# Talking-heads attention and a squared-ReLU FFN on one core: a new static schedule, 16-bit scaling of q, in-place ReLU, joined copies

## The chip, the core and the metric

The kernel runs on one core of one Trainium2 chip. Its engines each work off a queue of their own in program order: TensorE (PE: matmuls; its weight loads appear as PEld), VectorE (DVE), ScalarE (ACT), GpSimd (POOL) and SyncE (SP, which here only issues DMAs). They meet through semaphores. TensorE writes PSUM, which the kernel uses as eight banks of 128 x 512 fp32; DVE and ACT empty it into SBUF. The metric is the device time of one execution in microseconds.

## What is computed

```python
def _attn_ref(q, k, v, w_pre, w_post):              # q, k, v: (8, 12, 448, 64); w: (12, 12)
    scale = 1.0 / np.sqrt(q.shape[-1])
    scores = scale * np.matmul(q, k.transpose(0, 1, 3, 2))
    scores = np.einsum('bhij,hg->bgij', scores, w_pre)
    scores = scores - np.max(scores, axis=-1, keepdims=True)
    attn = np.exp(scores)
    attn = attn / (np.sum(attn, axis=-1, keepdims=True) + 1e-09)
    attn = np.einsum('bhij,hg->bgij', attn, w_post)
    return np.matmul(attn, v)

def reference(...):
    x = attn_out.transpose(0, 2, 1, 3).reshape(3584, 768)
    h = np.maximum(x @ w_in, 0.0)                   # w_in: (768, 2048), w_out: (2048, 768)
    return h * h @ w_out
```

Heads are mixed twice, once ahead of the softmax (`w_pre`) and once behind it (`w_post`).

## The kernel before

The eight batch entries are worked off one behind the other, each in these steps, which overlap with those of its neighbours:

- **T**: q and k come by DMA (issued by POOL, `load_qk`) and are transposed on TensorE (`emit_T`, L726) into `qkt`.
- **Scores**: for each pair of heads and 128 rows of q a score tile of 448 columns (`emit_QK`, L879) is copied from PSUM to `stage` (L486 on ACT, L487 on DVE: the helper `copy` does all plain copies), and a DMA (`emit_rel`, SP, L925) puts it in another order, with 5 rows x 12 heads on 60 partitions, into `dring`.
- **pre**: one small matrix on TensorE mixes the heads (`emit_pre`, L948). For the first 22 groups of ten rows of batch 0 the mix is made otherwise, without the DMA: DVE multiplies q by the 12 factors of `w_pre` (`emit_scale`, L802, "scaling"), and TensorE adds up the heads (`emit_direct`, L824).
- **Softmax**: ACT takes the exponential into `pring` and the row sums (`after_pre`, L965). DVE takes the reciprocal (`rinv`, L979). A **fold** multiplies the second mix's matrix `wk2b` by it into `wk2s` (L986), and a **tail** multiplies 64 columns of a pair's exponentials by it into `ptail` (L1001). `pring`, `wk2s` and `rinv` are rings of `NPS = 10`.
- **post**: the second mix, transposed at the same time (`emit_post`, L1036, L1050); its results leave PSUM as `a2t`.
- **AV** (L1120) gives `xt`. **F1** (L1176 in full rows, L1184 in half rows) gives the hidden layer: a ReLU from PSUM into one of three buffers `h1t` (L1213 on ACT, L1214 on DVE), then DVE squares it into `h2t` (L1223). **F2** (L1251 for the last tiles, L1303 full, L1311 half rows) gives the output through `osb` and a DMA that POOL issues (L1348).

TensorE uses its array in four forms: full (128 x 128), half rows, half columns, and quarters of 64 x 64, of which two or four run at once. Where TensorE would idle early on, the plan adds matmuls that compute nothing (L599).

The order on every engine is made ahead of time, while the program is built, by a planner (`_Plan.run`). It holds a list of tasks with their inputs, a cost for each engine that may do a task, and a priority. TensorE's tasks stand in ten streams (T, QK, pre, post, AV, direct, F1 twice, F2 twice), and the string `ORDER` says digit by digit which stream comes next. Tasks of engine `FLEX` go to ACT or DVE, wherever they would end first by the plan. A task of TensorE takes the PSUM banks that come free first. What stands in the order by the plan stays in that order on the chip; an engine waits at a task whose inputs are late, and all behind it with it. The plan's times come from constants:

```python
SEM_LAT = 60.0
MODE_SWITCH = 106.0                     # TensorE changes its array form
t_fold = add(..., DVE if g < 10 else POOL, fn_fold, ..., {POOL: (330.0, 370.0), DVE: (200.0, 280.0)}, ...)
```

`F1_FULL`, `F2_FULL`, `QK_QUAD` and `POST_QUAD` say, unit by unit, which array form is used.

Of the kernel before, what the change touches and what calls it, by code (L numbers as in the profile page):

```python
# [17 lines left out]
SEM_LAT = 60.0  # L18
MODE_SWITCH = 106.0
ACT_BIAS = 14.5  # L20
BLOCK = 256
# [11 lines left out]
    "0010155055051505511551555115555113553155550033555555550105555555311553332550220555315551"  # L33
    "2313332431244123622317667223677313361372267113667313242244137611376713127721266676623336"
    "7277128310028323839139229839200223444132622008111811181338317222167663123776313673132621"
    "4431411367217127766327621002677622383383338162267720028332677102208311813181338314212442"
    "2229391139313933922291444229119116316337221763363372217620016733722631620027137383200281"
    "1181118222939133911393124222441183138311831382224442216363372217633637212763362002277200"
    "2611637337339200292219119118131813183318222444223931193139331922244422881383138336221672"
    "1276200167337136336222772002736316720209119313922193831183138113822244422381381338224442"  # L40
    "2816336117117336221673373621167200226731362002713783382228382002911392219139393319222931"
    "9318338111811382224444442236171163377331722166662227637336372127922198338392298333832244"
    "42228876323267886673363363676787774448687787766676697767689989889999"
)
F1_FULL = "1111111111111111111111111111111100000000000001000000010000000110001010001111011111111111"
F2_FULL = "00000000000000000000000000101100"
QK_QUAD = "001000000001000000000000000000000000000000001001000000010000001000000000000000000000000000000000000000000000000000000000000000000000000000000000000000000000000"
POST_QUAD = "0000000000000000000000000000000000000000000000000000000000000000000000000000000000000000000000000000000000000000000000000000000000000000000000000000000000000000000000000000000001100000"
# [48 lines left out]
class _Group:  # L97


    __slots__ = ("n", "banks", "readers")  # L100

    def __init__(self, n):
        self.n = n
        self.banks = None
        self.readers = [[] for _ in range(n)]


class _Plan:
# [28 lines left out]
    def start(self):  # L137
        for t in self.tasks:
# [3 lines left out]
            for d in t.deps:  # L142
                if d.done:
                    t.avail = max(t.avail, d.end + SEM_LAT)
                else:
                    t.nwait += 1
                    d.succs.append(t)
# [50 lines left out]
    def _finish(self, t):  # L198
        t.done = True
        for s in t.succs:  # L200
            s.nwait -= 1
            spare = MARGIN.get((t.dma[0], s.engine), (0.0, 0.0)) if t.dma else (0.0, 0.0)
            s.avail = max(s.avail, t.end + SEM_LAT + spare[0 if t.end < 110e3 else 1])
# [53 lines left out]
    def bank_time(self, i):  # L257
        return max([t.end + SEM_LAT if t.done else INF for t in self.bank_users[i]] + [0.0])

    def find(self, n, now):  # L260
        best = sorted((max(self.bank_time(i), now), self.bank_age[i], i)
                      for i in range(len(self.bank_users)))
        return best[n - 1][0], [x[2] for x in best[:n]]
# [12 lines left out]
    def _commit_pe(self, t, start):  # L276
# [3 lines left out]
        if g is not None and g.banks is None:  # L280
            _, got = self.find(g.n, self.free[PE])
# [18 lines left out]
    def next_unit(self, order, at):  # L300
# [6 lines left out]
        if t.group is not None and t.group.banks is None:  # L307
            est = max(est, self.find(t.group.n, self.free[PE])[0])
# [43 lines left out]
def bass_talking_heads_attention__then__ffn_squared_relu_kernel(  # L352
# [45 lines left out]
    with ExitStack() as es:  # L398
# [7 lines left out]
        NPS = 10  # L406
        NOS = 2
        OP = F // 4
        NH1 = 3
# [10 lines left out]
        wq = sb("wq", [128, NP, H], DT.float32)  # L420
        wall = sb("wall", [128, NP, 2, H], DT.float32)
        mask2 = sb("mask2", [128, 2, H5], DT.float32)
# [6 lines left out]
        sb("align", [128, 224], DT.uint8)  # L429
# [13 lines left out]
        h1t = sb("h1t", [128, NH1, S], DT.bfloat16)  # L443
# [24 lines left out]
        def c_pe(t):  # L468
            return {PE: (t, t + 190.0)}
# [4 lines left out]

        def add(name, engine, fn, deps, cost, prio, mode=None, group=None, instrs=0):
            return plan.add(name, engine, fn, deps, cost, prio, "ctr", 1, mode, group=group,
# [11 lines left out]

        streams = [[] for _ in range(10)]
# [6 lines left out]
        def fn_init(eng, en):  # L496
# [4 lines left out]
            eng.memset(mask2[:, :, :], 1.0)  # L501
# [28 lines left out]
        t_m = select("init6", mask2, [[-64, 2], [-H, H5]], 0, 1, [t_init], -1e7 + 22)  # L530
        t_m = select("init7", mask2, [[64, 2], [H, H5]], H - 1, -1, [t_m], -1e7 + 23)
        t_mask2 = halves("init8", mask2, [t_m], -460.0)
# [13 lines left out]
        def fn_wsmall(eng, en):  # L546
            src = bass.AP(w_pre.tensor, 0, [[0, CH], [H, H], [1, H]])
            eng.dma_start(wrep[R0:R0 + NR, :], src).then_inc(sem_w0.handle, 16)
            for x in range(2):
                src = bass.AP(w_post.tensor, 0, [[0, H5], [H, H], [1, H]])  # L550
# [11 lines left out]
        for kk in range(2):  # L562
            def fn_wq(eng, en, r0=kk * 64, kk=kk):
                return eng.tensor_scalar(wq[r0:r0 + 64, :, :], wall[r0:r0 + 64, :, kk, :],
                                         scale, None, op0=ALU.mult)

            wq_of.append(add("wq%d" % kk, DVE, fn_wq, [t_wall], {DVE: (150.0, 220.0)}, -2e6))

        def fn_wk1(eng, en):
            o = wk1[:, 0:PR].rearrange("p (a b) -> p a b", b=H)  # L570
            i0 = wrep[:, :].unsqueeze(1).to_broadcast([128, H5, H])
            i1 = mask[:, 0, :].unsqueeze(2).to_broadcast([128, H5, H])
            return eng.scalar_tensor_tensor(o, i0, scale, i1, op0=ALU.mult, op1=ALU.mult)

        def fn_wk2(eng, en):
            r_ = None
            for x in range(2):
                r0, r1 = 64 * x, 64 * x + PR
                i0 = wrep2[r0:r1, :].unsqueeze(2).to_broadcast([PR, H, H5])
                i1 = mask2[r0:r1, 0, :].unsqueeze(1).to_broadcast([PR, H, H5])  # L580
# [6 lines left out]
        def warm_up(gap):  # L587
# [19 lines left out]
            start = max(now, t_warm.end + SEM_LAT, plan.find(1, now)[0])  # L607
# [102 lines left out]
        def emit_T(b):  # L710
            pb = b % 2
            for a in range(3):
                g = _Group(2)
# [767 lines left out]
```

## Time and profile before

| | us |
|---|---|
| three runs | 518.17, 518.59, 519.81 |
| their median | 518.59 |
| the profiled execution: from its first to its last instruction | 519.3 |
| TensorE busy in it | 506.3 |
| ACT, DVE, POOL busy | 434.1, 401.9, 268.4 |

The list of runs doesn't say which of them was profiled; its span lies 0.7 us above the median and 0.5 below the slowest. TensorE's granted clock was 1.00 throughout. In rows of the timeline a start and a duration in us stand first, then engine, line, operation and tiles; a bracket tells how long the engine had been idle and whom it waited for. In grouped rows (`x80 | 30.0, 405 | 1.9`) stand the count, busy us, mean ns of one, and idle us ahead. In rows of stages, `20.00:40.00`, the busy us of PE, PEld, DVE, ACT and POOL stand behind the length, with counts in brackets. In rows of waits stand the sum in us, the times and the longest. Rows of one operation that follow each other are merged: the duration of a merged row is that of all, and operations on one engine overlap a little, so the time from start to start is less than the mean of one.

### The profile page before, as it was taken

How to read it: one execution, taken by the hardware profiler on the slowest of the kernel's cores; microseconds unless marked ns; L12 is line 12 of the kernel's file. 1: busy time of each engine (PE TensorE's matmuls, PEld its weight loads, DVE VectorE, ACT ScalarE, POOL GpSimd, SP SyncE). 2: the span in 40 equal slices, each digit the busy share in tenths (PEclk: the TensorE clock that was granted, in tenths of full speed). 3: DMA queues.
4: the chain of work that ended last, by engine and by line, in shares of the span. 5: the costliest groups of instructions: out<-in, count | busy, mean ns of one | idle time of the engine just before them, and what ended most of it. 6: DMA issues, size and time to landing. Idle time of an engine off the chain costs nothing.

```text
span 519.3 us, 22377 instructions
## 1 busy us (share of the span) xinstructions
PE 506.3 (98%) x9169; PEld 319.7 (62%) x9169; DVE 401.9 (77%) x1025; ACT 434.1 (84%) x1256; POOL 268.4 (52%) x571
## 2 busy tenths in 40 slices
PE   7999899999999999999999999999999999999997
PEld 3455677567776664567455664566545665568884
DVE  8998999689979769888988869886896668755220
ACT  4989999799999898988888889888998888987531
POOL 9956556443673576244864459235664344443000
PEclk9999999999999999999999999999999999999999
DMA  8999999846895689646993679626995466551013
GB/s 112 196 227 193 199 180 189 168 115 136 157 190 135 142 174 187 124 97 141 173 186 76 142 156 197 148 66 152 174 166 119 102 154 120 103 118 32 1 32 93
DMA packets 83022, 72.33 MB, mean 139 GB/s; under 512 B 7160, under 2 KB 80424, under 8 KB 82920
## 3 DMA queue, kind: packets, MB, share of 16 engines
q0 software_dynamic: 37632, 33.83, 40.4%
q1 hardware_dynamic: 45000, 36.86, 29.0%
q8 instruction: 74, 1.21, 0.9%
q14 instruction: 28, 0.23, 0.1%
q10 hardware_dynamic: 288, 0.20, 0.1%
HBM read 47.27 MB, written 11.01 MB: 112 GB/s over the span
## 4 chain that ended last, share of the span: by engine, by line
PE 73%; DVE 12%; ACT 8%; DMA 3%; issue 2%; POOL 2%; POOLq 0%; ACTq 0%; DVEq 0%
PE ps L1311 23%; PE ps L1184 10%; PE ps L1176 10%; PE ps L1120 6%; PE ps L948 6%; PE ps L879 5%; PE ps L1036 5%; ACT pring L965 4%; PE ps L1303 3%; DVE stage L487 3%; DVE a2t L487 2%; PE ps L1251 2%; DMA kraw<-in_k_dram 2%; DVE w_out_sb L802 2%; PE ps L726 2%; ACT stage L486 2%
## 5 line engine op out<-in xcount | busy, mean ns | idle before, releaser
L965 ACT ACTIVATE pring<-ps 128x448 bf16<-128x448 f32 x360 | 191.7, 557 | 11.7 <-PE ps L948 9.4
L986 POOL TENSOR_TENSOR wk2s<-wk2b,rinv 128x120 bf16<-128x120 bf16 (+1 forms) x179 | 73.2, 409 | 145.7 <-DVE rinv L979 144.3
L487 DVE CAST a2t<-ps 128x420 bf16<-128x420 f32 (+1 forms) x208 | 124.8, 643 | 16.5 <-PE ps L1050 15.9
L1311 PE MATMUL ps<-w_out_sb,h2t 64*128 64x384 bf16 x1472 | 134.3, 323 | 0.3 <-ACT pring L965 0.2
L487 DVE CAST stage<-ps 128x448 bf16<-128x448 f32 (+1 forms) x179 | 107.3, 615 | 14.1 <-PE ps L879 12.8
L486 ACT ACTIVATE a2t<-ps 128x420 bf16<-128x420 f32 (+1 forms) x160 | 94.9, 645 | 13.1 <-PE ps L1050 12.8
L486 ACT ACTIVATE stage<-ps 128x448 bf16<-128x448 f32 (+1 forms) x181 | 94.8, 557 | 12.9 <-PE ps L879 12.2
L1311 PEld LDWEIGHTS ps<-w_out_sb,h2t 64*128 64x128 bf16 x1472 | 67.6, 94 | 45.3 <-issue 2.4
L1184 PE MATMUL ps<-xt,w_in_sb 64*128 64x448 bf16 (+1 forms) x840 | 88.4, 347 | 1.3 <-issue 1.1
L1348 POOL DMA_DIRECT2D out_dram<-osb x52 | 33.4, 648 | 93.3 <-ACT osb L486 30.7
L965 ACT ACTIVATION_READ_ACCUMULATOR pring<-ps 128x1 f32 x360 | 80.0, 222 | 0.0
L1176 PE MATMUL ps<-xt,w_in_sb 128*128 128x228 bf16 (+2 forms) x636 | 75.0, 270 | 1.0 <-ACT a2t L486 0.8
L1223 DVE TENSOR_TENSOR h2t<-h1t 128x448 bf16<-128x448 bf16 (+2 forms) x176 | 56.0, 341 | 20.2 <-ACT h1t L1213 17.1
L1001 POOL TENSOR_TENSOR ptail<-pring,rinv 128x128 bf16<-128x128 bf16 x171 | 70.2, 410 | 0.0
L1176 PEld LDWEIGHTS ps<-xt,w_in_sb 128*128 128x128 bf16 x636 | 58.2, 98 | 13.9 <-ACT a2t L486 1.7
L1036 PEld LDWEIGHTS ps<-wk2s,pring 60*128 60x128 bf16 (+1 forms) x2184 | 48.9, 94 | 24.7 <-issue 2.6
L1184 PEld LDWEIGHTS ps<-xt,w_in_sb 64*128 64x128 bf16 x840 | 37.5, 94 | 34.8 <-issue 2.2
L1213 ACT ACTIVATE h1t<-ps 128x448 bf16<-128x448 f32 (+2 forms) x100 | 43.5, 445 | 16.6 <-PE ps L1176 7.6
L1036 PE MATMUL ps<-wk2s,pring 60*128 60x60 bf16 (+1 forms) x2184 | 55.3, 187 | 1.3 <-ACT h1t L1213 0.6
L948 PE MATMUL ps<-dring,wk 64*64 64x448 bf16 (+1 forms) x676 | 54.0, 362 | 0.9 <-DVE a2t L487 0.3
L979 DVE RECIPROCAL rinv<-rowsum 128x2 f32<-128x2 f32 (+1 forms) x184 | 29.0, 157 | 32.9 <-ACT pring L965 31.5
L879 PE MATMUL ps<-qkt 64*128 64x448 bf16 (+1 forms) x372 | 51.1, 353 | 0.4 <-DVE qkt L487 0.3
(62 smaller groups left out, 564.1 us busy)
## 6 DMA issues: line engine op xcount, KB each, us to landing
dring<-stage SPq DMA_DIRECT2D x309, 105.0 KB
out_dram<-osb POOLq DMA_DIRECT2D x52, 192.0 KB, 4.0
vraw<-in_v_dram POOLq DMA_DIRECT2D x48, 128.0 KB
qraw<-in_q_dram POOLq DMA_DIRECT2D x48, 112.0 KB, 5.4
kraw<-in_k_dram POOLq DMA_DIRECT2D x48, 112.0 KB, 5.3
w_in_sb<-in_moe_w_in_dram POOLq DMA_DIRECT2D x8, 384.0 KB, 18.0
w_out_sb<-in_moe_w_out_dram POOLq DMA_DIRECT2D x8, 384.0 KB, 17.3
dring<-stage SPq DMA_DIRECT2D x30, 42.0 KB
```

Of the source, the lines that this page charges most:

```text
L486: return eng.activation(o, i_, AF.Copy)
L487: return eng.tensor_copy(o, i_)
L879: r_ = eng.matmul(ps[y * v:(y + 1) * v, g.banks[x], 0:S], qkt[r0:r0 + 64, pp, 0, j0:j0 + v], qkt[r0:r0 + 64, pp, 1 + pb, :], start=True, s ...
L948: r_ = eng.matmul(ps[64 * y:64 * y + 64, gr.banks[x], 0:S], wk1[64 * x:64 * x + 64 - R0 * x, :], dring[64 * x:64 * x + 64 - R0 * x, (g0 + ...
L965: return eng.activation(pring[:, pr, 0:S], ps[:, gr.banks[x], 0:S], AF.Exp, accum_out=rowsum[:, pr, :])
L986: return eng.tensor_tensor(wk2s[:, p0:p0 + n, :], i0.to_broadcast([128, n, PR]), rinv[:, p0:p0 + n, :].to_broadcast([128, n, PR]), ALU.mult)
L1001: return eng.tensor_tensor(ptail[:, p0 // 2, :, :], pring[:, p0:p0 + 2, 0:PJ], rinv[:, p0:p0 + 2, :].to_broadcast([128, 2, PJ]), ALU.mult)
L1036: r_ = eng.matmul(ps[z * v:(z + 1) * v, gr.banks[x], o0:o0 + PR], pring[64 * x:64 * x + PR, pr + y, c:c + v], wk2s[64 * x:64 * x + PR, pr ...
L1176: r_ = eng.matmul(ps[:, gs[ph].banks[0], 0:n], w_in_sb[:, ft, t * 128:(t + 1) * 128], xt[:, ft, c0:c1], start=(ft == 0), stop=(ft == NFT - 1))
L1184: r_ = eng.matmul(ps[:, gs[0].banks[x], 0:n], w_in_sb[64 * y:64 * y + 64, ft, t * 128:(t + 1) * 128], xt[64 * y:64 * y + 64, ft, c0:c1], s ...
L1223: return eng.tensor_tensor(h2t[:, t16, o0:o0 + n], h1t[:, s, 0:n], h1t[:, s, 0:n], ALU.mult)
L1311: r_ = eng.matmul(ps[:, gs[0].banks[hh], 0:FH], h2t[64 * y:64 * y + 64, t16, col:col + 128], w_out_sb[64 * y:64 * y + 64, t16, hh * FH:(hh ...
```

## The change

1. **Scaling of q in 16 bits.** The factors `wq` were fp32, one for each head, read with a step of 0; they are now bf16 and written out five times, and the product's columns stand in the order head, row instead of row, head. `wk1`, `mask2` and the loads of the weights follow that order; two of POOL's selections for `mask2` become two sums on DVE.
2. **In-place ReLU.** `h1t` goes; the ReLU writes `h2t`, and the square is taken there. The wait for the F2 of the batch before, which had stood at the square, stands at the ReLU.
3. **Joined copies.** A unit of TensorE may take two neighbouring banks (`_Group(2, True)`), and one instruction then empties both. The squares of a pair may be one instruction too.
4. **Folds and tails** may be on POOL or DVE, as the plan finds better, with 120 ns to DVE's disadvantage; before, those of the first ten groups were on DVE and all others on POOL.
5. **The planner's constants** are other ones, and `ORDER` and the strings of forms are new (`ENG_V` is all zeros and changes nothing). `NPS` goes from 10 to 12.

```diff
-SEM_LAT = 60.0
-MODE_SWITCH = 106.0
+LAT = {PE: 85.0, ACT: 32.0, DVE: 32.0, FLEX: 32.0, POOL: 78.0, SP: 60.0}
+DMA_LAT = 60.0
+MODE_SWITCH = 97.0
+FOLD_BIAS = 120.0
...
-    "0010155055051505511551555115555113553155550033555555550105555555311553332550220555315551"
+    "0010155505115500551155555555331555511355001155400155555315553315552355555550203552135551"
...
-        NPS = 10
+        NPS = 12
...
-        wq = sb("wq", [128, NP, H], DT.float32)
+        wq = sb("wq", [128, NP, H, H5], DT.bfloat16)
...
-                            "p (c a) -> p c a", a=H5).unsqueeze(3).to_broadcast(
-                            [128, 2 * n, H5, H])
-                        i1 = wq[:, p, :].unsqueeze(1).unsqueeze(1).to_broadcast(
-                            [128, 2 * n, H5, H])
+                            "p (c a) -> p c a", a=H5).unsqueeze(2).to_broadcast(
+                            [128, 2 * n, H, H5])
+                        i1 = wq[:, p, :, :].unsqueeze(1).to_broadcast(
+                            [128, 2 * n, H, H5])
...
+    def find(self, n, now, side=False):
+        if side:
+            t = [max(self.bank_time(i), now) for i in range(len(self.bank_users))]
+            e = min((max(t[i], t[i + 1]), max(self.bank_age[i], self.bank_age[i + 1]), i)
+                    for i in range(len(t) - 1))
+            return e[0], [e[2], e[2] + 1]
...
+        def two(g, c, dt=None):
+            a = g.banks[0]
+            return (ps if dt is None else dt)[:, a:a + 2, 0:c]
...
-            t_fold = add("fold%d_%d" % (b, c), DVE if g < 10 else POOL, fn_fold,
+            t_fold = add("fold%d_%d" % (b, c), FLEX, fn_fold,
                          [t_rec, t_wk2] + old_users(g),
-                         {POOL: (330.0, 370.0), DVE: (200.0, 280.0)},
+                         {POOL: (345.0, 391.0), DVE: (200.0, 283.0)},
...
+            t_fold.bias = FOLD_BIAS
...
+            def emit_relu(x, k, g, z):
+                h = h2t[:, t16 + x:t16 + x + k, o0:o0 + n]
+
+                def fn_relu(eng, en):
+                    i_ = two(g, n) if k == 2 else ps[:, g.banks[z]:g.banks[z] + 1, 0:n]
+                    if en == ACT:
+                        return eng.activation(h, i_, AF.Relu)
+                    return eng.tensor_scalar(h, i_, 0.0, None, op0=ALU.max)
+
+                t = add("relu%d_%d_%d" % (b, c0, t16 + x), FLEX, fn_relu,
+                        [ths[x if full else 1]] + free, c_ev(k * n), b * 1000.0 + 600)
```

Three places of the new order, by engine. In them `qkt` is the transposed q or k, `stage` the scores, `pring` the exponentials, `wk2s` a fold and `ptail` a tail; `w_out_sb` lends its space to the scaled q until its own weights are loaded.

DVE at the start of the program, from the factors of q to the sixth scaling, before:

```order
L564 TENSOR_SCALAR wq<-wall 64x72 x2
L487 COPY qkt<-ps 128x448
L802 TENSOR_TENSOR w_out_sb<-qkt,wq 128x8x60 x2
L487 COPY qkt<-ps 128x448
L802 TENSOR_TENSOR w_out_sb<-qkt,wq 128x8x60 x2
L487 COPY qkt<-ps 128x448 x2
L802 TENSOR_TENSOR w_out_sb<-qkt,wq 128x8x60 x2
```

and after:

```order
L617 TENSOR_SCALAR wq<-wall 64x360 x2
L579 TENSOR_REDUCE mask<-ident 60x5 x2
L528 COPY qkt<-ps 128x448
L864 TENSOR_TENSOR w_out_sb<-qkt,wq 128x8x60 x4
L528 COPY qkt<-ps 128x448
L864 TENSOR_TENSOR w_out_sb<-qkt,wq 128x8x60 x2
L528 CAST stage<-ps 128x448
```

The factors are wider, two sums stand ahead of the first copy of q, and four scalings instead of two ahead of the second copy.

ACT in the middle of batch 0's direct scores, behind its last plain copy of `qkt`, before:

```order
L486 ACTIVATE stage<-ps 128x448 x2
L965 ACTIVATE pring,rowsum<-ps 128x448 x2
L486 ACTIVATE stage<-ps 128x448
L965 ACTIVATE pring,rowsum<-ps 128x448 x2
L486 ACTIVATE stage<-ps 128x448 x2
L965 ACTIVATE pring,rowsum<-ps 128x448
L486 ACTIVATE stage<-ps 128x448 x2
L965 ACTIVATE pring,rowsum<-ps 128x448
```

and after:

```order
L527 ACTIVATE stage<-ps 128x896
L1032 ACTIVATE pring,rowsum<-ps 128x448 x6
L527 ACTIVATE a2t<-ps 128x2x84x5
L527 ACTIVATE stage<-ps 128x896
L1032 ACTIVATE pring,rowsum<-ps 128x448 x2
L527 ACTIVATE stage<-ps 128x896
L527 ACTIVATE stage<-ps 128x448 x2
L1032 ACTIVATE pring,rowsum<-ps 128x448
```

Six exponentials come in a row where four score copies had stood between them, and three of the copies empty two banks each.

POOL from the loads of the second batch entry's k on, before:

```order
L630 DMA kraw<-in_k_dram 64x2x448 x2
L641 DMA vraw<-in_v_dram 64x4x256 x6
L666 DMA w_in_sb<-in_moe_w_in_dram 128x3x512 x6
L986 TENSOR_TENSOR wk2s<-wk2b,rinv 128x120
L1001 TENSOR_TENSOR ptail<-pring,rinv 128x128
L986 TENSOR_TENSOR wk2s<-wk2b,rinv 128x120
L1001 TENSOR_TENSOR ptail<-pring,rinv 128x128
```

and after:

```order
L685 DMA kraw<-in_k_dram 64x2x448
L1053 TENSOR_TENSOR wk2s<-wk2b,rinv 128x120
L685 DMA kraw<-in_k_dram 64x2x448
L696 DMA vraw<-in_v_dram 64x4x256 x4
L1053 TENSOR_TENSOR wk2s<-wk2b,rinv 128x120
L696 DMA vraw<-in_v_dram 64x4x256 x2
L721 DMA w_in_sb<-in_moe_w_in_dram 128x3x512
L1053 TENSOR_TENSOR wk2s<-wk2b,rinv 128x120
L1069 TENSOR_TENSOR ptail<-pring,rinv 128x128
L721 DMA w_in_sb<-in_moe_w_in_dram 128x3x512 x5
L1053 TENSOR_TENSOR wk2s<-wk2b,rinv 128x120 x3
L1069 TENSOR_TENSOR ptail<-pring,rinv 128x128 x2
```

Three folds, which had been on DVE, stand between the loads, and the loads behind each wait for it.

272 lines of the change are left out of this document (171 added, 101 removed).

## The prediction

> **What bounds the kernel now.** I read the page's first part, then the waits of TensorE's queue, then its timeline at the waits, then the stages.
>
> ```profile
> span 519.3 us, 22377 instructions
> PE 506.3 (98%) x9169; PEld 319.7 (62%) x9169; DVE 401.9 (77%) x1025; ACT 434.1 (84%) x1256; POOL 268.4 (52%) x571
> 1.46 4.30 PE L599 MATMUL ps<-osb 128*128 128x448 bf16 x14 [1.46 <-DVE osb L584]
> 507.75 7.96 PE L1251 MATMUL ps<-w_out_sb,h2t 128*128 128x384 bf16 x48
> ```
>
> TensorE is busy for 506.3 of 519.3 us. Of the 13.0 that it is not, 1.46 lie ahead of its first matmul and 3.6 behind its last (507.75 + 7.96 = 515.7), so 8 us are gaps inside. All else hides behind it. The change can therefore act in three ways only: other streaming work on TensorE, other gaps, another start or end.
>
> Streaming first. The order of both programs has the same columns to stream: 12 two-tile score matmuls become 24 four-tile ones, one F1 unit passes from half rows (12 + 12) to full rows (12), 56 four-tile matmuls of post become 28 of two tiles, and nothing else differs. 48 matmuls back to back above take 7.96 us, which is (7.96 - 0.33) / 47 = 162 ns each, so these stream with no loss already. TensorE's work stays. What moves it are array forms: a unit of another form (full, half rows, half columns, quarters) costs a break.
>
> ```profile
> 9.84 0.93 PE L824 MATMUL ps<-qkt,w_out_sb 128*128 128x448 bf16 x4
> 10.70 0.41 PE L726 MATMUL ps<-ident,kraw 64*64 64x64 bf16 x28
> 27.12 4.71 PE L824 MATMUL ps<-qkt,w_out_sb 128*128 128x448 bf16 x24
> ```
>
> In the last row a 448-column matmul takes (4.71 - 0.35) / 23 = 0.19 us, so the four of the first end at 9.84 + 0.76 = 10.60, and the quarter form starts at 10.70: a break of 0.1 us. I counted 260 such breaks in the order of before and 269 in that of after: +0.9 us.
>
> **The gaps.** TensorE's own waits, longest first:
>
> ```profile
> PE ps L726 <- DMA kraw<-in_k_dram: 1.4, 2, 0.9
> PE ps L1184 <- issue: 1.1, 2, 0.9
> PE ps L1176 <- ACT a2t L486: 0.8, 1, 0.8
> PE ps L1036 <- ACT h1t L1213: 0.6, 1, 0.6
> PE ps L726 <- DMA qraw<-in_q_dram: 0.4, 1, 0.4
> PE ps L1036 <- POOL ptail L1001: 0.3, 1, 0.3
> ...
> 54.53 0.57 PE L948 MATMUL ps<-dring,wk 64*64 64x448 bf16 x8
> 55.67 0.34 PE L1036 MATMUL ps<-wk2s,pring 60*128 60x60 bf16 x12 [0.57 <-ACT h1t L1213]
> 61.90 0.19 PE L1050 MATMUL ps<-wk2b,ptail 60*128 60x60 bf16 x2
> 62.94 0.72 PE L1176 MATMUL ps<-xt,w_in_sb 128*128 128x220 bf16 x6 [0.85 <-ACT a2t L486]
> 110.02 0.38 PE L948 MATMUL ps<-dring,wk 64*64 64x448 bf16 x4 [0.31 <-DVE a2t L487]
> 451.50 1.80 PE L1311 MATMUL ps<-w_out_sb,h2t 64*128 64x384 bf16 x20
> ```
>
> Most name an engine that empties PSUM. A row's bracket is less than what is lost, since a matmul's end is modelled: two matmuls of 60 columns start at 61.90 and the next unit only at 62.94, so 0.9 us is lost after a break of 0.1. I went through all start times this way. After TensorE's warm-up, units that wait on a semaphore lose 2.1 us in 4 places up to 12.41, 0.4 in 5 from there to 46, 4.5 in 14 from 48.20 to 110.02, and 5.9 in 33 from there to the last at 451.50. Another 2.1 is lost inside units that wait for nothing ("issue" above). So 13 us in all could be won by a perfect order; what the change wins must come from them.
>
> **Part by part.** (1) The 16-bit scaling.
>
> ```profile
> 13.20 1.79 DVE L802 TENSOR_TENSOR w_out_sb<-qkt,wq 128x480 bf16<-128x480 bf16 x3
> L802 DVE TENSOR_TENSOR w_out_sb<-qkt,wq 128x480 bf16<-128x480 bf16 x24 | 14.9, 653 | 0.0
> L1223 DVE TENSOR_TENSOR h2t<-h1t 128x448 bf16<-128x448 bf16 x80 | 30.0, 405 | 1.9 <-ACT h1t L1213 1.4
> L1223 DVE TENSOR_TENSOR h2t<-h1t 128x228 bf16<-128x228 bf16 x48 | 13.3, 294 | 13.2 <-ACT h1t L1213 12.8
> 20.00:40.00 20.00, 19.86 (x320) 10.35 (x318) 19.79 (x49) 17.99 (x50) 13.23 (x19) 1.00 1.26 223
> 40.00:60.00 20.00, 18.83 (x357) 12.04 (x356) 17.21 (x47) 18.90 (x65) 13.97 (x31) 1.00 1.11 196
> ```
>
> Now one scaling holds DVE for (1.79 - 0.65) / 2 = 0.57 us. Products of two 16-bit operands cost (405 - 294) / 220 = 0.505 ns a column; 480 columns then last 294 + 252 x 0.505 = 421 ns, 0.23 less than 653. For 30 whole and 6 half ones that is 7 to 8 us off DVE up to 36 us. DVE is full there (third figure of the row from 20: 19.79 of 20), yet TensorE is too (19.86), so almost none is on TensorE's path in that stretch: the cover is the pipeline of scores that are ready. What it does is free DVE for evictions, and so ACT, which is the busier one in the next stretch (18.90 of 20), where the waits begin. The start: the wider factor table costs DVE two writes of 360 instead of 72 columns, some 0.3 us more each at a column a cycle, and two small sums stand behind it, all ahead of the first copy of q at 6.9; two scalings more stand ahead of the first copy of k. The faster scalings give about that back, so the first score products come no sooner than at 9.84. But TensorE's wait for q at 12.41 falls away, since six more score matmuls (6 x 0.19) now stand ahead of it: -0.4 (between +0.5, if the copies of k come late, and -0.8).
>
> (2) Joined copies.
>
> ```profile
> L486 ACT ACTIVATE qkt<-ps 128x448 bf16<-128x448 bf16 x5 | 2.7, 545 | 5.5 <-PE ps L726 5.5
> L486 ACT ACTIVATE qkt<-ps 128x896 bf16<-128x896 bf16 x5 | 4.6, 912 | 0.0
> 9.31 1.85 ACT L486 ACTIVATE stage<-ps 128x448 bf16<-128x448 f32 x4 [0.62 <-PE ps L879]
> 44.33 1.68 ACT pring L965 x6
> ```
>
> Separate ACT copies start every (1.85 - 0.56) / 3 = 0.43 us; a copy of double length adds 912 - 545 = 0.37. A join saves 0.06 us of ACT, and its 101 joins 6 us; DVE's 61, with about the same, 4. That is mostly hidden, but ahead of the first AV, ACT's queue is the chain (last row, of the chain of work): there the order of after has on ACT 22 instead of 26 stage copies (8 of them in 4 joins), 8 instead of 9 of a2t, one instead of two of qkt, and one more of q. By 0.43 to 0.5 each less the joins, about -3 us of ACT ahead of 50 us. The price: two banks stay held until one instruction ends, 0.37 us longer than with two engines at once. It is hidden while another of the eight banks is free.
>
> (3) Folds and tails.
>
> ```profile
> L986 POOL TENSOR_TENSOR wk2s<-wk2b,rinv 128x120 bf16<-128x120 bf16 x171 | 70.9, 415 | 142.3 <-DVE rinv L979 140.9
> L1001 POOL TENSOR_TENSOR ptail<-pring,rinv 128x128 bf16<-128x128 bf16 x171 | 70.2, 410 | 0.0
> L1001 DVE TENSOR_TENSOR ptail<-pring,rinv 128x128 bf16<-128x128 bf16 x5 | 1.5, 293 | 0.0
> 18.91 0.28 DVE L1001 TENSOR_TENSOR ptail<-pring,rinv 128x128 bf16<-128x128 bf16 x1
> 19.11 0.65 DVE L802 TENSOR_TENSOR w_out_sb<-qkt,wq 128x480 bf16<-128x480 bf16 x1
> ```
>
> 76 tails and 17 folds go to DVE, at 0.20 us of its queue each (18.91 to 19.11): +19 us, and POOL loses 93 x 0.41 = 38. DVE stays under TensorE: 401.9 - 8 - 4 + 19, less 3 for squares in pairs and about 10 for evictions that pass to ACT, is some 396. A pair's fold and tail then run side by side instead of one behind the other, so post can come 0.4 us sooner. POOL's releaser in row 1 shows that it waits for its input, not the input for it; TensorE waited for a tail once (0.3). So this is worth 0 to -1, I take -0.3 inside (5).
>
> (4) In-place ReLU: the wait for the last batch's F2 moves from the square to the ReLU, which holds PSUM. Queued behind it on ACT or DVE are exponentials and copies. But by the order F1 of a batch runs ahead of the end of the last batch's F2 only once (two units, batch 7; before: five), so it costs 0 to 0.3, and the wait of a ReLU for a free buffer goes:
>
> ```profile
> ACT h1t L1213 <- DVE h2t L1223: 3.1, 10, 0.4
> ```
>
> ACT had slack there. I take 0.
>
> (5) The new order with costs nearer to the rows (a break at 97 instead of 106 ns, folds dearer). Nothing in the trace prices it; its bounds are 0 and the 10.4 us of waits from 48 on, and below nothing, a new wait as large as the present ones. I take half of the 4.5 between 48 and 110, where ACT gets about 3 us less to do ahead of time, and a third of the 5.9 later, where ACT and DVE together carry as much as now: -2.2 and -2.0. Nearer to half than to all, since the 0.4 of idle matmuls at 47 us are in the new order too.
>
> Sum: -0.4 - 2.2 - 2.0 + 0.9 = **-3.7 us**. The span is 0.7 above the median of 518.59 that the three runs gave, and a difference carries over: **514.9**.
>
> **Rivals.** (A) The waits nearly all go: -0.8 for the start, -4.0 of the 4.5, -5.0 of the 5.9, +0.9 is -8.9, near 509.5. For it: no engine but TensorE is above 84%. Against: waits for loads and "issue" stay, and a static order can't fit every run.
>
> (B) Nothing to measure: the joins give back what the order wins. 0.37 us of longer holding, in 10 of some 160 joins on the path, is 3.7 us, and the time 518.6. For it: PSUM's emptying ends most waits. Against: two engines rarely take both halves at once when both are full.
>
> (C) Slower: folds starve on POOL behind DVE's products.
>
> ```profile
> 31.11 3.01 DVE L802 TENSOR_TENSOR h2t<-qkt,wq 128x480 bf16<-128x480 bf16 x6
> 31.30 3.06 POOL L986 TENSOR_TENSOR wk2s<-wk2b,rinv 128x120 bf16<-128x120 bf16 x1 [3.57 <-DVE rinv L979]
> 37.39 0.39 POOL L986 TENSOR_TENSOR wk2s<-wk2b,rinv 128x120 bf16<-128x120 bf16 x1 [1.48 <-DVE rinv L979]
> ```
>
> One fold took 3.06 us, as long as six scalings beside it, against 0.39 free. The first five folds and five tails of before stand on DVE, where they can't collide; in the new order six folds and three tails of the stage of scalings are on POOL, and three of these folds stand ahead of loads of k, v and w_in there. Each may come up to 2.7 late; a post waits in order on TensorE and all behind it. If three do, with 0.4 of slack each, that is 6.9 - 3.7 = +3.2, near 522. It decides from about 5.3 us of such waits on, where it eats the 3.7 and 1.6 more. Against: six scalings now last about 2 us, and the products stand less in a row. The Trainium skill states the mechanism (SBUF — State Buffer, section “SBUF: two separate sides”): a DVE operation with two SBUF inputs and a GpSimd one hold one port pair exclusively for a whole instruction. The rows at 31 us agree, one fold for a run of six. By that rule the 93 moved products, too, could each block POOL for about 0.28 us, 26 us in all on an engine that idles over 230; this would not show in the time by itself.
>
> **Chances.** Forecast 0.51 (511.5 to 517), A 0.14, B 0.19, C 0.16. A measurement of this kernel tells about 0.3%, 1.6 us, from no change: faster 0.65, same 0.19, slower 0.16. The range reaches from A's nearer half, 510.5, to C's lesser one, 520.5.
>
> **What would show it.** TensorE busy within 2 us of 506 in a span near 515.6; scalings near 0.4 us instead of 0.65; POOL near 230 busy, ACT and DVE within 10 of now; waits between 48 and 110 us halved, those named after a2t and h1t first. Wrong if posts wait for wk2s or ptail before 45 us (C), if units wait for joined copies (B), or if TensorE's busy time itself moves: then breaks or clocks were mispriced.

## The result: about 0.9% slower, and the profile after

| | before | after |
|---|---|---|
| runs, us | 518.17 to 519.81, median 518.59 | 522.52 to 525.24, median 524.23 (5 runs) |
| ratio, 95% interval | | 1.0078 (1.0052 to 1.0103) |
| the same again, later | 519.37 median of 11 | 524.64 median of 6, ratio 1.0109 (1.0081 to 1.0137) |
| profiled execution, span | 519.3 | 520.8 |

In every run that lists both, the time is some 1.75 us (1.67 to 1.86) above the span. So the profiled execution of before took about 521.0, one of its longer ones, and 520.8 to 519.3 understates the change. The lines of the page that answer to those of before:

```profile
span 520.8 us, 22005 instructions
PE 509.7 (98%) x9141; PEld 319.6 (61%) x9141; DVE 399.5 (77%) x999; ACT 439.4 (84%) x1169; POOL 238.7 (46%) x476
506.63 10.56 PE L1341 MATMUL ps<-w_out_sb,h2t 128*128 128x384 bf16 x64
```

The last matmul ends at 517.2, 3.6 us ahead of the end as before: TensorE is still all there is. DVE, ACT and POOL did what was forecast, and TensorE took longer over the same columns. Groups of instructions, with mean ns of one behind the comma:

```profile
L864 DVE TENSOR_TENSOR w_out_sb<-qkt,wq 128x480 bf16<-128x480 bf16 x24 | 9.8, 446 | 0.0
L1053 POOL TENSOR_TENSOR wk2s<-wk2b,rinv 128x120 bf16<-128x120 bf16 x155 | 69.1, 447 | 159.9 <-DVE rinv L1046 158.7
L1069 DVE TENSOR_TENSOR ptail<-pring,rinv 128x128 bf16<-128x128 bf16 x81 | 26.1, 322 | 1.5
```

A scaling takes 446 ns (653 before), a fold on POOL 447 (415), a tail on DVE 322 (293).

**Where TensorE lost time.** I measured it as in the prediction: for each matmul that waits on a semaphore, how much later it starts than streaming, or a break of 0.097 us, allows; only cases above 40 ns count. Means of four executions of the old order (before twice, `kept_both` and `before_redealt` below) and of two of the changed kernel:

| us of the execution | 0–13 | 13–46 | 46–115 | 115–260 | 260–520 | sum |
|---|---|---|---|---|---|---|
| old order | 2.1 | 0.7 | 3.8 | 3.0 | 3.1 | 12.6 |
| changed kernel | 1.4 | 2.6 | 4.4 | 3.5 | 2.1 | 13.9 |

Waits +1.3, nine more breaks +0.9, a first transposition that starts 1.05 us later because the idle matmuls ahead of it took longer, stalls without a wait some 0.2 less: 3.0 of the 3.2 us between the ends of the last matmul in these executions. What TensorE streams takes the same time on average, within 0.1 us. The rest of the difference between the medians lies in executions that were not profiled: the four of the old order took on average 1.3 us more than the medians of their kernels, the two of the new one 1.0 less. Where that lies, some 2.3 of the 5.6 us, no trace shows.

The largest new loss is in the second stretch. POOL, DVE and TensorE in the timeline of after:

```profile
23.50 2.49 POOL L1053 TENSOR_TENSOR wk2s<-wk2b,rinv 128x120 bf16<-128x120 bf16 x1 [0.18 <-DVE rinv L1046]
23.67 0.29 DVE L1069 TENSOR_TENSOR ptail<-pring,rinv 128x128 bf16<-128x128 bf16 x1
23.86 0.83 DVE L864 TENSOR_TENSOR w_out_sb<-qkt,wq 128x480 bf16<-128x480 bf16 x2
24.59 1.18 DVE L864 TENSOR_TENSOR h2t<-qkt,wq 128x480 bf16<-128x480 bf16 x3
24.51 0.55 PE L941 MATMUL ps<-qkt 64*128 64x448 bf16 x4
26.14 0.34 PE L1106 MATMUL ps<-wk2s,pring 60*128 60x60 bf16 x12 [1.08 <-ACT stage L527]
```

This is rival C's mechanism: a fold on POOL takes 2.49 us. Beside it DVE runs a tail and five scalings without a pause, until 25.77; the fold ends at 25.99, and the post behind it starts at 26.14, 1.24 us later than it could. The bracket names a copy on ACT that ended at 26.06, but the copy that the post waits for, the one ahead of two exponentials, had ended at 23.98. What had just ended was the fold. The Trainium skill (SBUF — State Buffer, section “SBUF: two separate sides”) has the loser of the shared port pair blocked for one whole instruction; here it was blocked for six in a row, as the fold at 31 us in before was, so in both cases the price was the length of the run.

The other new losses of the first stages come from the start:

```profile
1.46 5.17 PE L654 MATMUL ps<-osb 128*128 128x448 bf16 x14 [1.46 <-DVE osb L639]
6.43 0.92 DVE L617 TENSOR_SCALAR wq<-wall 64x360 bf16<-64x360 f32 x2
7.37 0.46 DVE L579 TENSOR_REDUCE mask<-ident 60x5 f32<-60x60 bf16 x2
7.86 0.39 DVE L528 COPY qkt<-ps 128x448 bf16<-128x448 bf16 x1
10.17 0.36 PE L941 MATMUL ps<-qkt 64*128 64x448 bf16 x2 [0.27 <-DVE qkt L528]
13.70 0.36 PE L941 MATMUL ps<-qkt 64*128 64x448 bf16 x2 [0.54 <-DVE qkt L528]
```

The wide factors and the two sums put the first copy of q at 7.86 instead of 6.89, and two score units wait for copies on DVE. The 14 idle matmuls of the first row took 4.30 us in before. With the transposition behind them 1 us later the load of k is no longer waited for (0.90 at 7.67 before), so the smaller waits up to 13 us in the table are no gain.

**What did come as forecast, and did not help.** Busy time by stage (PE, PEld, DVE, ACT, POOL), before and then after:

```profile
13.00:46.00 33.00, 32.86 (x488) 16.27 (x486) 31.29 (x78) 29.57 (x85) 24.54 (x40) 1.00 1.21 210
46.00:115.00 69.00, 66.00 (x1288) 46.77 (x1288) 58.72 (x166) 63.07 (x194) 40.43 (x89) 1.00 0.91 175
```

```profile
13.00:46.00 33.00, 31.06 (x487) 15.29 (x483) 26.39 (x72) 25.91 (x67) 21.15 (x33) 1.00 1.17 203
46.00:115.00 69.00, 66.87 (x1288) 46.50 (x1289) 59.41 (x157) 64.51 (x190) 36.80 (x75) 1.00 0.93 178
```

From 13 to 115 us ACT does 2.2 us less (about 3 were forecast) and DVE 4.2 less, while the waits from 46 to 115 stay at 4.3 (4.5 in before's first trace). All of this relief lies ahead of 46 us: behind it, where the waits are, ACT does 1.4 us more than before and DVE 0.7 more.

### The profile page after: what moved, and what is told of

Read it like the earlier page. It is cut to its first block, busy times and chain, and to the rows that moved or that the text cites. A ratio compares the mean times of both kernels' runs of the same rounds, so it can differ in the third digit from the quotient of the medians.

```text
span 520.8 us, 22005 instructions
## 1 busy us (share of the span) xinstructions
PE 509.7 (98%) x9141; PEld 319.6 (61%) x9141; DVE 399.5 (77%) x999; ACT 439.4 (84%) x1169; POOL 238.7 (46%) x476
## 4 chain that ended last, share of the span: by engine, by line
PE 83%; ACT 8%; DVE 7%; issue 1%; ACTq 0%; DVEq 0%
PE ps L1402 23%; PE ps L1262 14%; PE ps L1254 11%; PE ps L1015 7%; PE ps L1199 6%; PE ps L1106 6%; PE ps L941 5%; PE ps L886 4%; ACT pring L1032 3%; PE ps L1394 3%; ACT stage L527 2%; PE ps L1341 2%; DVE stage L528 2%; PE ps L782 2%; ACT a2t L527 2%; DVE w_out_sb L864 1%
## 5 line engine op out<-in xcount | busy, mean ns | idle before, releaser
L528 DVE CAST a2t<-ps 128x420 bf16<-128x420 f32 (+3 forms) x162 | 110.9, 720 | 22.2 <-PE ps L1120 21.9
L528 DVE CAST stage<-ps 128x448 bf16<-128x448 f32 (+3 forms) x152 | 103.1, 693 | 9.9 <-PE ps L941 8.4
L527 ACT ACTIVATE a2t<-ps 128x420 bf16<-128x420 f32 (+3 forms) x126 | 99.5, 840 | 10.7 <-PE ps L1120 10.0
L527 ACT ACTIVATE stage<-ps 128x448 bf16<-128x448 f32 (+3 forms) x143 | 89.9, 655 | 12.0 <-PE ps L941 11.1
L1262 PE MATMUL ps<-xt,w_in_sb 64*128 64x448 bf16 (+1 forms) x816 | 86.0, 347 | 0.2 <-DVE xt L528 0.2
L1106 PEld LDWEIGHTS ps<-wk2s,pring 60*128 60x128 bf16 x2160 | 47.3, 94 | 23.9 <-ACT stage L527 2.5
L1303 DVE TENSOR_TENSOR h2t<-h2t 128x448 bf16<-128x448 bf16 (+5 forms) x137 | 48.2, 373 | 16.6 <-ACT h2t L1290 16.3
L1106 PE MATMUL ps<-wk2s,pring 60*128 60x60 bf16 x2160 | 54.0, 187 | 2.1 <-ACT stage L527 1.1
L1290 ACT ACTIVATE h2t<-ps 128x228 bf16<-128x228 f32 (+3 forms) x97 | 44.8, 471 | 10.7 <-PE ps L1254 7.4
L1199 PEld LDWEIGHTS ps<-a2t,vraw 128*64 128x64 bf16 x960 | 38.6, 109 | 5.4 <-ACT osb L527 2.4
```

Of the source, the lines that this page charges most:

```text
L527: return eng.activation(o, i_, AF.Copy)
L528: return eng.tensor_copy(o, i_)
L1106: r_ = eng.matmul(ps[z * v:(z + 1) * v, gr.banks[x], o0:o0 + PR], pring[64 * x:64 * x + PR, pr + y, c:c + v], wk2s[64 * x:64 * x + PR, pr ...
L1199: r_ = eng.matmul(po, vraw[:, h, sl, :], m, start=(k == 0), stop=(k == NS))
L1262: r_ = eng.matmul(ps[:, gs[0].banks[x], 0:n], w_in_sb[64 * y:64 * y + 64, ft, t * 128:(t + 1) * 128], xt[64 * y:64 * y + 64, ft, c0:c1], s ...
L1303: return eng.tensor_tensor(h, h, h, ALU.mult)
```

## The experiments

Two kinds. Those **planned anew** change one thing in the source and let the planner deal out the work again under a given `ORDER`. Those with a **kept list** replace `plan.run(ORDER)` by a table of all tasks, in the order in which the planner had committed them, each with its engine and its banks; the five engines' programs and their waits then stay as they were, but for what the diff names. The diffs are shortened, and some lines tell a list or a string in words. All ratios are to before on the same chip.

| kernel | median us | ratio (95%) | breaks | lost in waits (one trace) |
|---|---|---|---|---|
| before, beside each of four groups of these kernels | 518.6, 519.7, 518.6, 519.4 | 1 | 260 | 12.7 and 11.7 (two traces) |
| `kept_both` | 518.55 | 0.9996 (0.9981–1.0011) | 260 | 12.3 |
| `before_redealt` | 519.78 | 1.0018 (1.0004–1.0032) | 260 | 13.5 |
| `before_relu` | 523.02 | 1.0071 (1.0044–1.0099) | 260 | 14.1 |
| `before_flexfolds` | 524.92 | 1.0103 (1.0075–1.0132) | 260 | 16.7 |
| `oldorder_foldsold` | 526.01 | 1.0123 (1.0091–1.0156) | 260 | 17.3 |
| `oldorder` | 528.86 | 1.0189 (1.0165–1.0214) | 262 | 20.8 |
| changed, `after_again` | 524.64 | 1.0109 (1.0081–1.0137) | 269 | 14.0 |
| `kept_mended` | 522.99 | 1.0081 (1.0058–1.0103) | 269 | 14.4 |
| `kept_split` | 524.32 | 1.0098 (1.0072–1.0124) | 269 | 14.5 |
| `kept_split_all` | 524.27 | 1.0099 (1.0080–1.0118) | 269 | 15.6 |
| `folds10` | 525.82 | 1.0134 (1.0095–1.0172) | 269 | 15.4 |
| `after_redealt` | 528.09 | 1.0174 (1.0147–1.0202) | 269 | 20.3 |
| `nojoin` | 528.91 | 1.0187 (1.0162–1.0212) | 269 | 21.7 |
| `foldsold` | 531.74 | 1.0226 (1.0195–1.0258) | 269 | 21.6 |

Over all kernels the time roughly follows the last column: 9 us more of waits from `kept_both` to `nojoin` go with 10 us more of time. For the change itself the column says little: 14.0 against 11.7 and 12.7, with 5 us more of time.

### First: one part at a time, planned anew

**before_again**, the kernel before, for a second trace.

> The kernel before, once more, for a second trace of it. Its first trace has a span of 519.3 us, but the changed kernel's runs tell more by 1.75 us than their spans (522.55 to 520.8), and the runs of the kernel before have a median of 518.59. Theory 1: the first trace is of an unusually long execution, and this one has a span near 516.9, with the loss that lies in the difference (some 2.4 us) in units that wait for nothing (the first trace has 2.1 us of that, 1.1 of them at 206.8). Rival: the span is near 519 again, and the changed kernel's time around its span is another one.

It took 519.86 us, span 518.1, so the time is 1.75 above the span here too. The span of 516.9 did not come: its losses in waits are those of the first trace within 1 us, and those without a wait are as large, some 2 us, but stand elsewhere (last section).

**folds10**: the folds and tails of the first ten groups back on DVE, in the changed kernel.

```diff
-            t_fold = add("fold%d_%d" % (b, c), FLEX, fn_fold,
+            t_fold = add("fold%d_%d" % (b, c), DVE if g < 10 else FLEX, fn_fold,
```

(and the same for the tails). A joined copy into `qkt` for the second batch entry also waits for the scalings of both its pairs, not of one, here and in `foldsold`.

> The changed kernel with folds and tails of the first ten groups on DVE, as before; all others as the plan likes. Theory 1 (a fold starves on POOL behind DVE's products: 2.49 us at 23.5, and TensorE's post comes 1.24 us late at 26.1): the wait at 26 goes, and 1.2 to 2 us with it: 522 to 523 of 524.2. Theory 2 (the new order with its breaks and waits all over costs it): under 0.5 us changes, the time stays near 524. Theory 3 (the start, where the wider factors and two sums delay the first copy of q by 1 us, carries it): the wait at 26 goes, but others come in its place, and the time stays within 0.7.

The wait at 26 us is gone, but the total is no shorter, 525.82: there is a new loss of 1.76 us without a wait at 19.5, and 2.5 us more of waits behind 260. The planner moved 34 pieces to another engine, not only the folds and tails of the first groups, so this run doesn't price the starved fold by itself.

**oldorder**: the changed code with the `ORDER` and the array forms of before, no joins.

```diff
-ORDER, F1_V, QK_V, POST_V, F2_V, T_V of after
+ORDER and the form strings of before; no digit of 2 or 3
```

> The changed kernel's code (16-bit scaling, in-place ReLU, folds and tails on either engine, the new constants, rings of 12) with the old order of TensorE's units and the old forms, and so with no joined copy. Theory 1 (folds starving at the start): they still may go to POOL there, so 1 to 2 us above 518.6, about 520. Theory 2 (the new order costs it): 518 to 519, like before, or less by up to 2 for the shorter scalings. Theory 3 (the start): TensorE's first score product comes at 10 us instead of 8.9 here too, and the time is 519.5 to 521.

**nojoin**: the changed kernel with its new order, every digit for a joined copy reduced by 2.

```diff
-F1_V = "33313133...", QK_V = "00102022...", POST_V = "22222200..."
+F1_V = "11111111...", QK_V = "00100000...", POST_V = "00000000..."
```

> The changed kernel in the new order, each joined copy or square again as two. Theory 4 (joined copies hold two banks longer, and that costs it): 520 to 522. Theory 2 (the order itself): 524 or more, since the order was made for the joined ones. Theory 1: the wait at 26 us stays if the second fold stays on POOL, and the time within 1 of 524.

Both are at 528.9, slower than the changed kernel itself. So this new order fits its own joins and its own rules better than the old one does; that does not say why it is slower than before.

**foldsold**: folds and tails placed as before, in the changed kernel (`DVE if g < 10 else POOL`).

> The changed kernel in its new order with its joined copies, folds and tails placed as before: DVE for the first ten groups, POOL for all others. Theory 5 (the 76 tails and 17 folds on DVE, 19 us of its queue, are what costs it: evictions come later, and TensorE waits for banks at many places by 0.1 to 0.6 us): DVE is busy for about 375 to 385 us, TensorE's busy time falls from 509.7 towards 506, and the time is 517 to 521. Rival 2 (the order itself and its nine more breaks): 524 or more, since the order was made for the other placing, and posts wait for POOL.

531.74, the slowest of all. DVE fell to 385.8 us busy and that bought nothing:

```profile
span 530.0 us, 21994 instructions
PE 511.8 (97%) x9141; PEld 318.6 (60%) x9141; DVE 385.8 (73%) x910; ACT 437.0 (82%) x1165; POOL 266.0 (50%) x569
```

In this plan 14 us less on DVE gain nothing. But beside 101 folds and tails 109 other pieces changed engine, so what the moved folds cost in a kept order is not shown by it.

**oldorder_foldsold**: like `oldorder`, with the folds placed as before as well; what is left of the change is the scaling, the in-place ReLU, `NPS = 12` and the constants.

> The changed code in the old order, without joins, and with folds and tails placed as before: what is left of the change is the scaling, the in-place ReLU, the rings of 12 and the planner's constants. Theory 5: near 518 to 521, against 528.9 with folds on either engine. Rival 6 (the constants make the plan worse, since with 32 ns instead of 60 it counts on inputs too early): 524 to 529 still. Rival 7 (the in-place ReLU holds PSUM): 522 to 526.

**before_flexfolds**: the kernel before with free folds and tails.

```diff
-            t_fold = add("fold%d_%d" % (b, c), DVE if g < 10 else POOL, fn_fold,
+            t_fold = add("fold%d_%d" % (b, c), FLEX, fn_fold,
+            t_fold.bias = 120.0
```

> The kernel before, with one part of the change: folds and tails on POOL or DVE as the plan likes, with the change's costs and its 120 ns to DVE's disadvantage. Theory 5: the same load goes to DVE, and the time rises by 4 to 9 us, to 523 to 528. Rivals 6 and 7: it stays within 2 us of 518.6.

**before_relu**: the kernel before with the in-place ReLU and square.

```diff
-                    return eng.activation(h1t[:, s, 0:n], ps[:, g.banks[x], 0:n], AF.Relu)
+                    return eng.activation(h, ps[:, g.banks[x], 0:n], AF.Relu)   # h = h2t[...]
```

> The kernel before with the in-place ReLU alone. Theory 5: within 1 us of 518.6, since F1 runs ahead of the end of the last F2 only twice. Rival 7: 520 to 524.

526.01, 524.92, 523.02: put into a plan that was made without them, these parts cost 3.3 to 6.3 us by the medians, though TensorE's order stays the same, unit for unit. In `before_relu` 55 of some 3,700 tasks changed engine, in `oldorder_foldsold` 105, in `before_flexfolds` 246. From these runs alone one can't tell whether the instruction or the new dealing costs the time. That needed the kept lists.

### Second: the instructions without the planning

**kept_both**: the list of before, with the 16-bit scaling and the in-place ReLU put in.

```diff
-        per_engine, _ = plan.run(ORDER)
+        per_engine, _ = plan.replay(PLAN)     # tasks, engines and banks of the kernel before
...
-                    return eng.activation(h1t[:, s, 0:n], ps[:, g.banks[x], 0:n], AF.Relu)
+                    return eng.activation(h, ps[:, g.banks[x], 0:n], AF.Relu)
```

> The order of all five engines, the engine of every piece, the banks and the waits are those of the kernel before, written out as a fixed list and not planned anew; in it the scalings are the 16-bit ones and the ReLU is in place (but for four ReLUs, which the list has ahead of the reads that they would overwrite and which keep the separate buffer), the second half of the wider wq table stands behind the first copy of q, and two small selects on POOL go. If the loss comes from planning anew around cheaper instructions and not from them, the time is that of the kernel before or a little less: 517.5 to 519.0. If the instructions themselves cost the time (in-place writes, wide sums at the start), it is 521 to 523, as it was for the in-place ReLU planned anew.

518.55 against 518.56, ratio 0.9996 (0.9981 to 1.0011). This clears the scaling and the in-place ReLU (but for four), with the second half of the wide factors behind the first copy of q, and it shows as plainly that they gain nothing:

```profile
span 517.4 us, 22306 instructions
PE 506.3 (98%) x9169; PEld 320.0 (62%) x9169; DVE 396.2 (77%) x1025; ACT 433.5 (84%) x1256; POOL 264.9 (51%) x569
```

DVE has 5.7 us less to do than before, TensorE's busy time is the same to 0.1 us.

**before_redealt**: before, planned anew with the handicap of ACT in the choice of engines moved.

```diff
-ACT_BIAS = 14.5
+ACT_BIAS = 20.0
```

> The kernel before with one number of its planner moved, ScalarE's handicap in the choice of an engine, from 14.5 to 20 ns: 12 pieces change engine, no instruction becomes dearer or cheaper, TensorE's order stays. Theory that the order is fitted to one dealing of the copies: 1 to 3 us slower, 519.6 to 521.6. Rival, that only changes of cost matter: 518.6 within 0.5.

12 tasks change engine: ratio 1.0018 (1.0004 to 1.0032), 0.2 to 1.7 us. Expected were 1 to 3; re-dealing 12 tasks costs a little, at the edge of what can be measured.

**after_redealt**: the same edit in the changed kernel.

> The changed kernel with the same number moved from 14.5 to 20 ns: 57 pieces change engine. If its order fits its own dealing on the chip as closely as the old one did, it loses 3 to 5 us, 527 to 529. If the fit that it was searched for is not there on the chip, the dealing does not matter: 523.5 to 525.5.

57 tasks change engine: 528.09, ratio 1.0174, 3.4 to 5 us more than the changed kernel. The first theory had 527 to 529. Both orders are thus fitted to one dealing, and that of the changed kernel is real on the chip. Why its fit is worse than the old one's, these runs don't show.

### Third: what the new list loses

**kept_mended**: the changed kernel's list, with three places mended.

```diff
-fold0_5, fold0_7 on pool; wq1 and init8 (the sums) ahead of the first copy of q
+fold0_5, fold0_7 on dve; wq1 behind that copy, init8 just ahead of wk2
```

> The list of the changed kernel, kept as it is but for three places: the folds of the pairs at chunks 4 and 6 of the first block are on DVE in place of POOL, the second half of wq stands behind the first copy of q, and the two reduces for the mask stand just ahead of their user at 18 us. Theory: the changed kernel runs 2.6 us behind its own plan by 36 us and hardly more behind it later, and four steps make that up (0.33 and 0.63 at the second and third score products, 0.35 and 1.24 at the second mixes of chunks 2 and 4); with them mended the time is 521.7 to 522.7. Rival: what is won by 36 us is lost again in waits behind it, 524.

The mend of the fold works where it is. DVE, then TensorE:

```profile
23.42 0.26 DVE L1446 TENSOR_TENSOR wk2s<-wk2b,rinv 128x120 bf16<-128x120 bf16 x1
21.38 0.34 PE L1499 MATMUL ps<-wk2s,pring 60*128 60x60 bf16 x12 [0.63 <-DVE ptail L1462]
24.64 0.33 PE L1499 MATMUL ps<-wk2s,pring 60*128 60x60 bf16 x12
...
155.30 0.38 PE L1408 MATMUL ps<-dring,wk 64*64 64x448 bf16 x4
156.30 0.38 PE L1408 MATMUL ps<-dring,wk 64*64 64x448 bf16 x4 [0.61 <-DMA dring<-stage]
```

The fold takes 0.26 us and its post stands at 24.64 instead of 26.14. The post ahead of it now loses 0.79 instead of 0.34 (second row). The second score unit no longer waits, but the third still does, 0.52 us at 12.96 for a copy on DVE, so that wait comes from the order of DVE's pieces and not from the wide factors and sums. By 130 us the program is 0.9 ahead of the changed kernel. Then a pre has to wait 0.61 for a transfer into `dring` that the later program had found landed, and nearly all is given back. The median, 522.99, lies between the theory's 521.7 to 522.7 and the rival's 524; the ratio, 1.0081, stands against 1.0078 and 1.0109 of the changed kernel, so the gain is between nothing and some 1.5 us. Of the loss 4.4 us (3.0 to 5.3 by the interval) stay.

**after_again**, the changed kernel, timed beside the next two.

> The changed kernel as it is, beside the two below and timed with them: 522.5 to 524.5.

**kept_split**: the list of the changed kernel, 51 joined copies of `a2t` on ACT issued as two.

```diff
-            how = int(POST_V[len(post_units)])
+            how = int(POST_V[len(post_units)]) - (2 if g0 in APART else 0)
```

> The list of the changed kernel, kept; only the 51 joined copies of mixed weights that stand on ScalarE are two copies of half the width, one behind the other in the same place on the same engine. In the trace of the changed kernel such a joined copy holds ScalarE for 1004 ns from its start to the next one's, and a single copy of half the width for 502, so the engine's time should not change, and the first of the two banks is free some 0.5 us sooner. If banks held longer by joined copies cost the 3 to 4 us, this is 520 to 522; if they cost nothing, 522.5 to 524.5.

**kept_split_all**: every joined copy, ReLU and square issued as two, in its place.

> As the last one, but every joined copy (206 with the squares) is two of half the width in the same place on the same engine. ScalarE and VectorE get some 0.06 to 0.07 us more of work for each of the others, 7 to 9 us in all over the two. If joining pays by engine time, this is 2 us or more slower than the changed kernel, 525 to 528; if it pays nothing, or costs by the banks, 520 to 524.5.

524.64, 524.32, 524.27: no difference, though one of up to some 1.5 us can't be excluded. The traces hold something else. In both split kernels the fold ahead of 26 us no longer starves: it starts at 23.49 and 23.53, the tail on DVE at 23.68 and 23.72 (23.67 in the changed kernel), the fold takes 0.49 us, the tail some 0.46, and the post stands at 24.91. So a few hundredths of a us seem to decide whether rival C's case happens, and the 1.24 us that go there do not show in the time.

`kept_split_all` and `nojoin` have the same pieces and the same order on TensorE; 373 of 3,707 pieces stand on another engine, and the queues of DVE, ACT and POOL and the PSUM banks differ with them. The one takes 524.27 us (1.0099), the other 528.91 (1.0187). Both are given against before on their own chip. The 4.6 us are the price of one dealing against another, with no piece changed.

What joined copies save is small; in groups of the changed kernel's trace:

```profile
L527 ACT ACTIVATE a2t<-ps 128x840 bf16<-128x840 f32 x49 | 56.3, 1155 | 8.1 <-PE ps L1120 7.6
L527 ACT ACTIVATE a2t<-ps 128x420 bf16<-128x420 f32 x69 | 43.2, 669 | 2.5 <-PE ps L1120 2.3
```

1155 is not far from twice 669, and from the start of one to that of the next it is 1004 ns for the joined and 502 for the single copy (medians of those that follow without a pause): no saving at all for this copy.

So scaling and ReLU together, and the joins, are worth about nothing in a kept order, and by elimination the order and the dealing are left: 9 more breaks, two late score units, a starved fold, and small waits spread over the rest. For the 93 moved folds and tails that is argued only: no kept list has them back, but for two folds in `kept_mended`. The planner's constants and `NPS` were not run by themselves. No version here beats the kernel before; `kept_both` equals it. Not tried was a new search of the order that prices a POOL fold by what runs beside it.

## Why the prediction was wrong

514.9 us was forecast, 524.2 came.

- **Term (5), the new order: -4.2 forecast.** This is the step that failed. It took half of the waits from 48 to 110 us and a third of the later ones, on the ground that ACT would have 3 us less to do. ACT had 2.2, all ahead of 46 us, and DVE more, but the waits went from 3.8 to 4.4 and from 6.1 to 5.6. `kept_both` shows that the ground was wrong: 5.7 us less on DVE in the old places are worth 0.2 ± 0.8 us. `kept_split_all` and `nojoin` show what counts in its place, which piece stands where: the same work, dealt otherwise, differs by 4.6 us. Why this order has more waits than the old one stays open.
- **The bounds of (5)** allowed a new wait "as large as the present ones", but the estimate left out new waits where there had been none. From 13 to 46 us they rose from 0.7 to 2.6.
- **Rival C** happened, once and not three times: 1.24 us at 26 us. It had been given 0.16 and "near 522". It goes away in `kept_split` and `kept_split_all` with no change of the time, and mending it and the start gains between nothing and 1.5 us of the 5.6, so it is a small part of the result at most.
- **Rivals A and B**: the waits rose, so A is out. B's time did not come, and splitting all joins in their place, which frees the first of two banks sooner, changes nothing (1.0099 against 1.0109). Two engines at once, which B compared with, ran only in `nojoin`, under another dealing.
- **Part (2)**: a join was to save ACT 0.06 us. For copies of scores it does (0.81 against 2 x 0.44 from start to start), for those of `a2t` it saves nothing.
- **The start, -0.4**: the waits up to 13 us fell by 0.7, but only because the idle matmuls ended 1 us later. The copies of q and k came later, as the upper bound of that term had it, and score units wait for them at 10.17 and 13.70. Nothing of the 0.4 shows.
- **Sizes**: the span's 0.7 us above the median did not tell where the profiled execution lay, since a time is some 1.75 above its span. A's sum, -8.9, gives 509.7 and not 509.5; nothing hangs on it.
- **Right**: no change of streaming work; 269 breaks for 260, +0.9; scalings near 0.4 (446 ns); DVE 399.5 against "some 396" and POOL 238.7 against "near 230"; the in-place ReLU at 0 (in `kept_both`, with the scalings).

## What to carry to other kernels

Where a static order was searched for one exact set of costs, its value lies in the fit of every queue to every other, and an edit that makes the planner deal again can throw it away (0.2% for 12 pieces here, 0.9% for 373): compare an edit in a kept list first, and only then let a planner use it. Free time on an engine that is not the bound was worth nothing by itself here; to forecast a gain, name the unit that waits and the piece that will now come sooner. And a POOL operation beside a run of two-input DVE products is to be priced by the length of that run, with a chance: in two of the traces it got in first.

## What the runs showed of the hardware

TensorE sometimes stops inside a unit that waits for nothing. The kernel before in its second trace, and then the changed kernel in its second trace:

```profile
197.94 0.74 PE L1184 MATMUL ps<-xt,w_in_sb 64*128 64x448 bf16 x6
199.93 0.74 PE L1184 MATMUL ps<-xt,w_in_sb 64*128 64x448 bf16 x6 [1.26 <-issue]
```

```profile
100.05 0.81 PE L1402 MATMUL ps<-w_out_sb,h2t 64*128 64x384 bf16 x8
102.02 0.83 PE L1402 MATMUL ps<-w_out_sb,h2t 64*128 64x384 bf16 x8 [1.16 <-issue]
```

In the changed kernel's first trace the same unit streamed through. Such stalls of up to 1.8 us came to between 0 and about 3.5 us per execution, at other places each time, so one trace against another can be wrong by more than 1 us; only the medians of several runs carry a difference of this size. Their cause stays open.

The idle matmuls at the start follow each other by 0.37 us at first and by 0.19 from some moment on. In the two traces of before 8 and 7 of the first 14 are slow, in those of the changed kernel 13 and 14, in `before_relu` 14 and in `oldorder` 8; the granted clock reads 1.00 in all six. Whether the kernel has a part in it is not shown.
